# Windowed attention with sinks and a maxout FFN on one core: row-tiled scores, values by one head, transposes by DMA, and one ring of eight PSUM banks

## The chip, the cores and the metric

The kernel runs on one core of a Trainium2 chip. The metric is the device time of one execution in microseconds (us), as the median of a few runs. The engines are called TensorE (PE in the profile, its weight loads PEld), VectorE (DVE), ScalarE (ACT), GpSimd (POOL) and SyncE (SP, which only issues DMAs here).

## The reference

There are 4 batches, 8 heads, 768 positions and 64 numbers per head. Each query sees the 128 positions up to its own and the first four positions (the sinks). The attention's output goes through an FFN whose hidden layer is the largest of three products.

```python
scores = (1.0 / np.sqrt(D)) * np.matmul(q, k.transpose(0, 1, 3, 2))
pos = np.arange(S)
rel = pos[:, None] - pos[None, :]
keep = (pos[None, :] < 4) | ((rel >= 0) & (rel < 128))
scores = np.where(keep, scores, -1000000000.0)
a = np.exp(scores - np.max(scores, axis=-1, keepdims=True))
a = a / (np.sum(a, axis=-1, keepdims=True) + 1e-09)
x = np.matmul(a, v).transpose(0, 2, 1, 3).reshape(4 * 768, 512)
h = np.maximum(np.maximum(x @ w1, x @ w2), x @ w3)      # 512 -> 768
out = h @ w_out                                         # 768 -> 512
```

All inputs and the output are float32. The kernel computes in bfloat16 with sums in float32.

## The kernel before

The work is cut into 12 chunks of 256 positions, three in each batch, so chunks 0, 3, 6 and 9 begin a batch. A chunk's attention reads its own keys and values and the last 128 of the chunk before. Chunks that begin a batch need neither those nor the sinks. Four pairs of heads are handled in a chunk.

`load` (L59) fetches a chunk of Q, K and V in float32 on SP's queue: four DMAs of 256 KB for Q and K (L70) and four of 128 KB for V (L75). GpSimd casts them to bfloat16 (L167 for Q and K, L175 for V); the first two chunks of Q and K are cast by VectorE. `prep` transposes Q or K of two pairs of heads on TensorE (L192); ScalarE copies the transposed Q out of PSUM (L195) and VectorE the transposed K (L200), with small copies for the sinks' keys (L208).

K is kept padded. The 128 columns of a stationary tile are 64 keys of one head and 64 of the other, and each head's 64 rows are zero in the other's half. `zeros` (L94 to L99) clears these halves, and those of V, mostly on GpSimd. With it one matmul of 128 rows gives the scores of both heads of a pair for 64 keys each. `score` (L222 to L226) makes two such tiles for a pair, ScalarE takes the exponentials (L232), and VectorE multiplies by a mask of zeros and ones (L234). Scores of the sinks (L240, L244) of all heads are made in one tile with the keys padded in the same way.

`av` multiplies these by V with a column of ones, so that the last column is the sum of the weights (L253 for the sinks, L263 for the rest, 130 columns for two heads). VectorE divides (L268 the reciprocal, L271 the product). `xpose` transposes the result on TensorE (L282) and ScalarE copies it (L283). `ffn_h` makes a tile of 256 hidden numbers for one of the three weight matrices in eight matmuls (L294). The first matrix is copied by ScalarE (L298); VectorE takes the maximum with the other two (L300). `ffn_y` makes 128 rows of the output in six matmuls of 512 columns (L305), ScalarE copies (L308), and SP stores.

PSUM has eight banks in three pools: two for scores, two for transposes and values, and four for the FFN. The order of all work is written out by hand as a string of steps, where K, Q, S, Z, A, T, F and Y stand for the functions above and the letter after them for the chunk:

```python
for i in range(2, NCH):
    if i + 2 < NCH:
        cast(i + 2)
    if i + 3 < NCH:
        load(i + 3)
    run("Sb0 Fa0 Sb1 Kc0 Fa1 Sb2 Kc1 Fa2 Sb3 Fa3 Zb Sb4 Fa4 Ab00 Sb5 Fa5 Ab01 Sb6 Qc0 Fa6 "
        "Sb7 Qc1 Fa7 Fa8 Ab10 Ab11 Ya0 Tb0 Tb1 Ya1", a=i, b=i + 1, c=i + 2)
```

So an iteration holds the FFN of one chunk, the attention of the next and the transposes of Q and K of the one after. The attention of chunks 0 to 2 and the FFN of chunks 0 and 1 stand ahead of the loop, in the same manner. The weights are loaded with a cast by DMAs on GpSimd's queue (`load_w`, L129, and `load_wo`, L138), in program order with GpSimd's other work.

Of the kernel before, what the change touches and what calls it, by code (L numbers as in the profile page):

```python
# [16 lines left out]
def kernel(  # L17
# [31 lines left out]
    with tc.manual_schedule():  # L49
# [3 lines left out]
        ps_s = tc.alloc_tile_pool(name="ps_s", bufs=2, space=bass.MemoryType.PSUM)  # L53
        ps_o = tc.alloc_tile_pool(name="ps_o", bufs=2, space=bass.MemoryType.PSUM)
        ps_f = tc.alloc_tile_pool(name="ps_f", bufs=4, space=bass.MemoryType.PSUM)

        raws = {}

        def load(ci, gate=None):  # L59

            b, c = divmod(ci, CPB)
            t0 = c * 256
            eng = nc.sync
            qk = raw.tile([128, 2, H, 2, D], F32, tag="qk_raw", name="qk_raw")
            vr = raw.tile([128, 2, NP, 2, D], F32, tag="v_raw", name="v_raw")
            if gate is not None:
                gate.memset(qk[0:1, 0, 0, 0, 0:1], 0.0)
            for g in range(2):
                for j, src in ((0, k), (1, q)):
                    eng.dma_start(  # L70
                        out=qk[:, j, 4 * g:4 * g + 4],
                        in_=src[b, 4 * g:4 * g + 4, t0:t0 + 256].rearrange("h (p i) d -> p h (i d)", i=2))
            for h in range(2):
                for n in range(2):
                    eng.dma_start(  # L75
                        out=vr[64 * h:64 * h + 64, n],
                        in_=v[b, h::2, t0 + 128 * n:t0 + 128 * n + 128]
                            .rearrange("a (r i) d -> r a (i d)", i=2))
            raws[ci] = (qk, vr)

        load(0)
        vs_raw = const.tile([H * n_sink, B, D], F32, name="vs_raw")
        for h in range(H):
            nc.sync.dma_start(out=vs_raw[h * n_sink:(h + 1) * n_sink],
                              in_=v[:, h, 0:n_sink].rearrange("b s d -> s b d"))


        kb_sb = [const.tile([128, CPB, 2, NP, 2, 128], BF16, name=f"kb{i}") for i in range(2)]
        qT = [const.tile([128, NP, S], BF16, name=f"qT{i}") for i in range(2)]
        vb_sb = [const.tile([128, CPB, 2, NP, 2, 2, D + 1], BF16, name=f"vb{i}") for i in range(2)]  # L90
        ks = [const.tile([128, NP * 136], BF16, name=f"ks{i}") for i in range(2)]
        vs = const.tile([128, B, H, D + 1], BF16, name="vs")

        def zeros(i, c, eng):  # L94
            for h in range(2):
                hp = slice(64 * h, 64 * h + 64)
                eng.memset(kb_sb[i][hp, c, :, :, :, 64 - 64 * h:128 - 64 * h], 0.0)  # L97
                eng.memset(vb_sb[i][hp, c, :, :, :, 1 - h], 0.0)
                eng.memset(vb_sb[i][hp, c, :, :, :, h, D:D + 1], 1.0)  # L99

        zeros(0, 0, nc.vector)
        nc.vector.memset(ks[0], 0.0)
        nc.vector.memset(ks[1], 0.0)

        ident = const.tile([128, 128], BF16, name="ident")
        make_identity(nc, ident)

        msk = const.tile([128, 2, 4, 128], BF16, name="msk")
        nc.gpsimd.memset(msk[:, :, 0:2], 1.0)
        for h in range(2):  # L110
            hp = slice(64 * h, 64 * h + 64)
            nc.gpsimd.affine_select(
                out=msk[hp, :, 1], in_=msk[hp, :, 1], compare_op=ALU.is_ge, fill=0.0,
                base=0, pattern=[[-1, 2], [1, 128]], channel_multiplier=-2)
            nc.gpsimd.affine_select(
                out=msk[hp, :, 0], in_=msk[hp, :, 0], compare_op=ALU.is_gt, fill=0.0,
                base=0, pattern=[[1, 2], [-1, 128]], channel_multiplier=2)
        nc.gpsimd.tensor_copy(msk[:, :, 2:4], msk[:, :, 0:2])
        msk0 = const.tile([128, 2, 3, 128], BF16, name="msk0")
        nc.gpsimd.tensor_copy(msk0, msk[:, :, 1:4])  # L120
        for h in range(2):
            nc.gpsimd.memset(msk0[64 * h:64 * h + n_sink // 2, :, 0:2], 1.0)

        w_sb = {}

        def load_w(fo, fn):
            for wi, w in enumerate((moe_w1, moe_w2, moe_w3)):
                wt = const.tile([128, DS, fn], BF16, name=f"w{wi}_{fo}")
                nc.gpsimd.dma_start(  # L129
                    out=wt, in_=w[:, fo:fo + fn].rearrange("(a p) f -> p a f", p=128))  # L130
                for f in range(fn // 128):
                    w_sb[wi, fo // 128 + f] = wt[:, :, f * 128:(f + 1) * 128]
# [3 lines left out]
        def load_wo():  # L136
            for a in range(2):
                nc.gpsimd.dma_start(  # L138
                    out=wo[:, 3 * a:3 * a + 3],
                    in_=moe_w_out[384 * a:384 * a + 384].rearrange("(a p) f -> p a f", p=128))  # L140


        R = H * n_sink
        bm = const.tile([R, H], F32, name="bm")

        def sink_v_init():
            nc.gpsimd.memset(bm, 1.0)
            nc.gpsimd.affine_select(out=bm, in_=bm, compare_op=ALU.is_ge, fill=0.0, base=0,
                                    pattern=[[-n_sink, H]], channel_multiplier=1)
            nc.gpsimd.affine_select(out=bm, in_=bm, compare_op=ALU.is_ge, fill=0.0,  # L150
                                    base=n_sink - 1, pattern=[[n_sink, H]], channel_multiplier=-1)
            nc.gpsimd.memset(vs, 0.0)

        def sink_v(b):
            nc.gpsimd.tensor_tensor(
                out=vs[0:R, b, :, 0:D],
                in0=vs_raw[:, b].unsqueeze(1).to_broadcast([R, H, D]),
                in1=bm.unsqueeze(2).to_broadcast([R, H, D]), op=ALU.mult)
            nc.gpsimd.tensor_copy(vs[0:R, b, :, D:D + 1], bm.unsqueeze(2))

        bfs = {}

        def cast_qk(ci, j, g, eng):
            qk = raws[ci][0]
            if ci not in bfs:
                bfs[ci] = raw.tile([128, 2, 2, 2, 256], BF16, tag="qk_bf", name="qk_bf")
            eng.tensor_copy(  # L167
                bfs[ci][:, j, g].rearrange("p i (h d) -> p h i d", d=D),
                qk[:, j, 4 * g:4 * g + 4])

        def cast_v(ci, h):
            b, c = divmod(ci, CPB)
            vr = raws[ci][1]
            hp = slice(64 * h, 64 * h + 64)
            nc.gpsimd.tensor_copy(  # L175
                vb_sb[b % 2][hp, c, :, :, :, h, 0:D].rearrange("p n a i d -> p (n a i) d"),
                vr[hp].rearrange("p n a i d -> p (n a i) d"))

        def cast(ci):
            for j, g in ((0, 0), (1, 0), (0, 1), (1, 1)):  # L180
                cast_qk(ci, j, g, nc.gpsimd)
            for h in range(2):
                cast_v(ci, h)

        def prep(ci, j, g):

            b, c = divmod(ci, CPB)
            x = bfs[ci]
            pt = ps_o.tile([128, 2, 2, 128], BF16, tag="o", name="pt")
            for i in range(2):  # L190
                for p in range(2):
                    nc.tensor.transpose(pt[:, i, p], x[:, j, g, i, p * 128:(p + 1) * 128], ident)  # L192
            if j == 1:
                dst = qT[b % 2][:, 2 * g:2 * g + 2, c * 256:c * 256 + 256]
                nc.scalar.copy(dst.rearrange("p a (t i) -> p i a t", i=2), pt)  # L195
            else:
                kb = kb_sb[b % 2]
                for h in range(2):
                    hp = slice(64 * h, 64 * h + 64)
                    nc.vector.tensor_copy(  # L200
                        kb[hp, c, :, 2 * g:2 * g + 2, :, 64 * h:64 * h + 64]
                            .rearrange("p i a n r -> p i (a n) r"),
                        pt[hp].rearrange("p i a (n r) -> p i (a n) r", r=64))
                if c == 0:
                    kv = ks[b % 2].rearrange("p (a y) -> p a y", y=136)
                    for h in range(2):
                        for i in range(2):
                            nc.vector.tensor_copy(  # L208
                                kv[:, 2 * g:2 * g + 2, 4 * h + i:4 * h + 4:2],
                                kb[:, 0, i, 2 * g:2 * g + 2, 0, 64 * h:64 * h + 2])  # L210

        es = {}

        def score(ci, s):
            b, c = divmod(ci, CPB)
            p, i = divmod(s, 2)
            kb = kb_sb[b % 2]
# [161 lines left out]
        for i in range(2, NCH):  # L379
            if i + 2 < NCH:  # L380
                cast(i + 2)
# [42 lines left out]
```

## Time and profile before

| What | Value |
|---|---|
| median of 3 runs | 237.17 us (236.94 to 238.38) |
| profiled execution: span | 235.6 us |
| TensorE busy | 203.3 us, 86% |
| VectorE, ScalarE, GpSimd busy | 140.4, 115.1, 91.8 us |
| DMA | 28.66 MB, 122 GB/s over the span |

The span is the time from the first to the last instruction of the profiled execution, and the median holds what lies around it too, so the two differ by 1.6 us. Busy shares are means over stages that have different limits: the start, where weights and the first chunks arrive, the loop over chunks, and the last chunk. Matmuls are pipelined, so the mean length of one holds its latency, and the distance from one to the next is shorter.

### The profile page before, as it was taken

How to read it: one execution, taken by the hardware profiler on the slowest of the kernel's cores; microseconds unless marked ns; L12 is line 12 of the kernel's file. 1: busy time of each engine (PE TensorE's matmuls, PEld its weight loads, DVE VectorE, ACT ScalarE, POOL GpSimd, SP SyncE). 2: the span in 40 equal slices, each digit the busy share in tenths (PEclk: the TensorE clock that was granted, in tenths of full speed). 3: DMA queues.
4: the chain of work that ended last, by engine and by line, in shares of the span. 5: the costliest groups of instructions: out<-in, count | busy, mean ns of one | idle time of the engine just before them, and what ended most of it. 6: DMA issues, size and time to landing. Idle time of an engine off the chain costs nothing.

```text
span 235.6 us, 4953 instructions
## 1 busy us (share of the span) xinstructions
PE 203.3 (86%) x1956; PEld 163.9 (70%) x1968; DVE 140.4 (60%) x314; ACT 115.1 (49%) x213; POOL 91.8 (39%) x129
## 2 busy tenths in 40 slices
PE   0647876989944999999899999998999999999993
PEld 0434655877533868978778869877978689799781
DVE  7737674456342973855856739729629648547350
ACT  2622363257450457546446555464564466473411
POOL 8599961699468650621602502603404300000000
PEclk9999999999997999999999999999999999999998
DMA  6599199682699904907607519139039020010202
GB/s 171 101 134 239 32 161 259 118 120 58 182 278 233 232 18 142 218 3 234 122 22 236 105 63 266 30 101 251 10 107 248 4 89 4 25 66 0 92 0 89
DMA packets 46006, 28.66 MB, mean 122 GB/s; under 512 B 2208, under 2 KB 42912, under 8 KB 45984
## 3 DMA queue, kind: packets, MB, share of 16 engines
q1 hardware_dynamic: 42016, 25.21, 43.4%
q0 software_dynamic: 3968, 3.15, 9.0%
q8 instruction: 15, 0.25, 0.5%
q14 instruction: 7, 0.06, 0.1%
HBM read 25.20 MB, written 6.29 MB: 134 GB/s over the span
## 4 chain that ended last, share of the span: by engine, by line
PE 57%; DVE 13%; POOL 9%; DMA 7%; ACT 5%; issue 4%; SPq 3%; POOLq 0%; DVEq 0%; ACTq 0%
PE h_ps L294 29%; PE y_ps L305 10%; PE o_ps L263 6%; DMA v_raw<-in_v_dram 4%; DVE e_sb L234 4%; DVE h_sb L300 4%; DMA w<-in_moe_w_dram 3%; PE st L224 3%; ACT e_sb L232 3%; PE pt L192 2%; DVE kb L200 2%; PE xt_ps L282 2%; POOL vb L175 2%; SPq L70 2%; POOL kb L97 2%
## 5 line engine op out<-in xcount | busy, mean ns | idle before, releaser
L294 PE MATMUL h_ps<-xT,w 128*128 128x256 bf16 x864 | 111.0, 278 | 2.2 <-DMA w<-in_moe_w_dram 1.5
L294 PEld LDWEIGHTS <-w 128*128 128x128 bf16 x864 | 82.7, 100 | 13.1 <-DMA w<-in_moe_w_dram 2.0
L232 ACT ACTIVATE e_sb<-st 128x512 bf16<-128x512 f32 (+1 forms) x96 | 53.5, 564 | 44.2 <-PE st L226 44.2
L234 DVE TENSOR_TENSOR e_sb<-e_sb,msk 128x1024 bf16<-128x1024 bf16 (+1 forms) x48 | 36.6, 762 | 56.0 <-ACT e_sb L232 55.9
L300 DVE TENSOR_TENSOR h_sb<-h_sb,h_ps 128x512 bf16<-128x512 bf16 x72 | 49.3, 685 | 15.6 <-PE h_ps L294 13.3
L167 POOL CAST qk_bf<-qk_raw 128x512 bf16<-128x512 f32 x40 | 24.9, 627 | 82.0 <-DMA qk_raw<-in_k_dram 71.1
L263 PE MATMUL o_ps<-vb,e_sb 128*128 128x130 bf16 x352 | 30.8, 227 | 6.8 <-DVE e_sb L234 4.0
L305 PE MATMUL y_ps<-wo,h_sb 128*128 128x512 bf16 x132 | 32.7, 379 | 0.6
L263 PEld LDWEIGHTS <-e_sb 128*128 128x128 bf16 x352 | 24.8, 100 | 10.5 <-DVE e_sb L234 6.2
L308 ACT COPY y_sb<-y_ps 128x512 f32<-128x512 f32 x24 | 14.0, 585 | 35.6 <-PE y_ps L305 32.1
L175 POOL CAST vb<-v_raw 64x1024 bf16<-64x1024 f32 x24 | 26.5, 1104 | 9.5 <-DMA v_raw<-in_v_dram 6.1
L192 PE MATMUL pt<-ident,qk_bf 128*128 128x128 bf16 x192 | 19.4, 230 | 12.1 <-DVE qk_bf L167 5.5
L298 ACT CAST h_sb<-h_ps 128x512 bf16<-128x512 f32 x36 | 21.1, 585 | 15.8 <-PE h_ps L294 15.6
L224 PE MATMUL st<-qT,kb 128*128 128x256 bf16 x96 | 27.0, 285 | 1.6 <-ACT qT L195 0.8
L200 DVE COPY kb<-pt 64x512 bf16<-64x512 bf16 x48 | 20.1, 419 | 6.9 <-PE pt L192 6.3
L192 PEld LDWEIGHTS <-qk_bf 128*128 128x128 bf16 x192 | 13.6, 102 | 14.4 <-POOL qk_bf L167 7.1
L195 ACT COPY qT<-pt 128x512 bf16<-128x512 bf16 x24 | 17.7, 737 | 11.5 <-PE pt L192 11.5
L226 PE MATMUL st<-qT,kb 128*128 128x128 bf16 x96 | 21.9, 228 | 0.0
L271 DVE TENSOR_TENSOR x_sb<-o_ps,rc 128x256 bf16<-128x256 f32 x48 | 20.4, 425 | 1.7
L305 PEld LDWEIGHTS <-h_sb 128*128 128x128 bf16 x144 | 13.0, 98 | 11.9 <-DVE h_sb L300 1.2
L283 ACT COPY xT<-xt_ps 128x512 bf16<-128x512 bf16 x24 | 13.2, 595 | 9.0 <-PE xt_ps L282 9.0
L222 PE MATMUL st<-qT,kb 128*128 128x128 bf16 x64 | 14.0, 218 | 0.9 <-ACT qT L195 0.8
(43 smaller groups left out, 130.7 us busy)
## 6 DMA issues: line engine op xcount, KB each, us to landing
qk_raw<-in_k_dram SPq DMA_DIRECT2D x24, 256.0 KB
qk_raw<-in_q_dram SPq DMA_DIRECT2D x24, 256.0 KB
v_raw<-in_v_dram SPq DMA_DIRECT2D x48, 128.0 KB
out_dram<-y_sb SPq DMA_DIRECT2D x24, 256.0 KB
w<-in_moe_w_dram POOLq DMA_DIRECT2D x3, 512.0 KB, 7.4
w<-in_moe_w_dram POOLq DMA_DIRECT2D x3, 256.0 KB, 4.9
wo<-in_moe_w_out_dram POOLq DMA_DIRECT2D x2, 384.0 KB, 5.6
vs_raw<-in_v_dram SPq DMA_DIRECT2D x8, 4.0 KB
```

Of the source, the lines that this page charges most:

```text
L167: eng.tensor_copy(bfs[ci][:, j, g].rearrange("p i (h d) -> p h i d", d=D), qk[:, j, 4 * g:4 * g + 4])
L175: nc.gpsimd.tensor_copy(vb_sb[b % 2][hp, c, :, :, :, h, 0:D].rearrange("p n a i d -> p (n a i) d"), vr[hp].rearrange("p n a i d -> p (n a ...
L192: nc.tensor.transpose(pt[:, i, p], x[:, j, g, i, p * 128:(p + 1) * 128], ident)
L200: nc.vector.tensor_copy(kb[hp, c, :, 2 * g:2 * g + 2, :, 64 * h:64 * h + 64] .rearrange("p i a n r -> p i (a n) r"), pt[hp].rearrange("p i ...
L224: nc.tensor.matmul(st[:, 1:3], lhsT=kb[:, c, i, p, 0], rhs=qh[:, q0:q0 + 256], start=True, stop=True)
L226: nc.tensor.matmul(st[:, 3], lhsT=kb[:, c, i, p, 1], rhs=qh[:, q0 + 128:q0 + 256], start=True, stop=True)
L232: nc.scalar.activation(e[:, i, lo:], st[:, lo:], AF.Exp, scale=scale)
L234: nc.vector.tensor_mul(e[:, :, lo:], e[:, :, lo:], msk if c > 0 else msk0)
L263: nc.tensor.matmul(o[:, 2 * a:2 * a + 2], lhsT=es[ci, p][:, i, sl], rhs=vb_sb[b % 2][:, n // 2, n % 2, p, i], start=(c == 0 and x == 0), s ...
L294: nc.tensor.matmul(hp[:, f], lhsT=w_sb[wi, 2 * fp + f][:, ds], rhs=xTs[ci][:, ds, :], start=(ds == 0), stop=(ds == DS - 1))
L300: nc.vector.tensor_max(dst, dst, hp)
L305: nc.tensor.matmul(yp, lhsT=hs[ci][:, fb, t * 128:(t + 1) * 128], rhs=wo[:, fb], start=(fb == 0), stop=(fb == FB - 1))
```

## The change

The kernel is written anew on the same chunks. Its parts:

- **Layout.** Each DMA of Q, K or V takes a whole chunk (512 KB). A partition holds two neighbouring positions. K and Q are kept without padding, transposed, in rings of four chunks (`kT`, `qT`), V in a ring of four (`vb`).
- **Scores.** For each head of a pair a matmul uses 64 rows of TensorE (rows 0 to 63 or 64 to 127) and gives 128 keys of one head. The two heads' matmuls alternate and write to two banks.
- **Values.** A matmul covers 128 keys of one head and has 65 columns. Four tiles of PSUM (one for each pair) are held open through a chunk's values, both halves of 128 queries in one tile.
- **Sinks.** Their scores are four matmuls on 32 columns of TensorE each, their values matmuls on 32 rows each. The sinks' V is gathered by a matmul with a selection matrix (`sink_v`), no longer by DMAs.
- **Transposes.** Q and K of chunks 0 to 2 and x of chunks 0 to 2 go through TensorE. From chunk 3 on, Q and K are transposed by four DMAs a chunk (`turn_dma`) and x by one (`xpose_dma`), all on SP's queue.
- **PSUM.** One pool of eight banks serves every tile in turn.
- **Start.** Loads of chunks 0 and 1 are issued at once (Q of chunk 0 on ScalarE's queue), each weight matrix is one DMA, and the masks are built in half the size first.
- **Stores.** A chunk is stored by two DMAs.

```diff
-        ps_s = tc.alloc_tile_pool(name="ps_s", bufs=2, space=bass.MemoryType.PSUM)
-        ps_o = tc.alloc_tile_pool(name="ps_o", bufs=2, space=bass.MemoryType.PSUM)
-        ps_f = tc.alloc_tile_pool(name="ps_f", bufs=4, space=bass.MemoryType.PSUM)
+        psum = tc.alloc_tile_pool(name="psum", bufs=8, space=bass.MemoryType.PSUM)
+        def bank(shape, dtype, name):
+            return psum.tile(shape, dtype, tag="b", name=name)
+        RING = 4
+        kT = [const.tile([128, 2, NP, 2, 64], BF16, name=f"kT{i}") for i in range(RING)]
+        qT = [const.tile([128, 2, NP, 2, 64], BF16, name=f"qT{i}") for i in range(RING)]
+        vb = [const.tile([128, 2, H, D + 1], BF16, name=f"vb{i}") for i in range(RING)]
...
+        def turn_dma(ci, w):
+            dst = (kT if w == "k" else qT)[ci % RING]
+            x = bfs[ci, w].rearrange("q p i a d -> q (p i a d)")
+            for n in range(2):
+                nc.sync.dma_start_transpose(
+                    out=dst[:, n].rearrange("q p i r -> q (p i) r"), in_=x[64 * n:64 * n + 64])
...
+        def score(ci, pairs):
+            b, c = divmod(ci, CPB)
+            kc, qc = kT[ci % RING], qT[ci % RING]
+            for p in pairs:
+                st = [bank([128, 4, 128], F32, "st") for a in range(2)]
+                for s, x, n, q0, q1 in ((0, kT[(ci - 1) % RING], 1, 0, 1), (1, kc, 0, 0, 2),
+                                        (3, kc, 1, 1, 2)):
+                    if s == 0 and c == 0:
+                        continue
+                    for a in range(2):
+                        hp = slice(64 * a, 64 * a + 64)
+                        nc.tensor.matmul(
+                            st[a][:, s:s + q1 - q0],
+                            lhsT=x[hp, n, p].rearrange("q i r -> q (i r)"),
+                            rhs=qc[hp, q0:q1, p].rearrange("q n i r -> q n (i r)"),
+                            start=True, stop=True)
...
+        def expo(ci, p):
+            lo = 0 if ci % CPB else 1
+            e, st = es[ci, p]
+            for a in range(2):
+                nc.scalar.activation(e[:, a, lo:], st[a][:, lo:], AF.Exp, scale=scale)
+            nc.vector.tensor_mul(e[:, :, lo:], e[:, :, lo:], msk0 if lo else msk)
...
+        def av_open(ci):
+            b, c = divmod(ci, CPB)
+            for p in range(NP):
+                os_[ci, p] = bank([128, 2, 2, D + 1], F32, "o")
+            if c:
+                for t in range(2):
+                    for p in range(NP):
+                        hp = slice(32 * p, 32 * p + 32)
+                        nc.tensor.matmul(
+                            os_[ci, p][:, t], lhsT=es[ci, "sink"][hp, t], rhs=vs[b % 2][hp],
+                            start=(t == 0), stop=False, skip_group_check=True,
+                            tile_position=(32 * p, 0))
...
+                    for s, cv, n in blocks:
+                        nc.tensor.matmul(
+                            o[:, t, a], lhsT=e[:, a, s], rhs=vb[cv % RING][:, n, 2 * p + a],
+                            start=first, stop=True, skip_group_check=True)
+                        first = False
...
+        def xpose_dma(ci):
+            xTs[ci] = work.tile([128, 2, DS, 128], BF16, tag="xT", bufs=3, name="xT")
+            nc.sync.dma_start_transpose(
+                out=xTs[ci].rearrange("q t s r -> q (t s) r"),
+                in_=xs[ci].rearrange("q t p a d -> q (t p a d)"))
...
+        masks()
+        for g in range(2):
+            for w in "kq":
+                cast_qk(0, w, g, nc.vector)
+                turn(0, w, g)
+            score(0, range(2 * g, 2 * g + 2))
+            for p in range(2 * g, 2 * g + 2):
+                expo(0, p)
...
+        load_w(0)
+        load_w(1)
+        sink_init()
+        sink_k(0)
+        masks_late()
+        for g in range(2):
+            cast_qk(1, "k", g, nc.vector)
+            cast_qk(1, "q", g, nc.gpsimd)
+        load_w(2)
...
+        load_wo()
+        av_open(0)
...
+        cast(3)
+        load(4)
+        for p in range(NP):
+            expo(2, p)
+            if p < 2:
+                ffn_y(0, p)
+        store(0)
+        turn_dma(3, "k")
+        turn_dma(3, "q")
...
         for i in range(2, NCH):
+            n = i + 1
+            last = n >= NCH
+            cast(i + 2)
+            load(i + 3)
+            if i + 2 < NCH:
+                turn_dma(i + 2, "k")
+                turn_dma(i + 2, "q")
+            if not last:
+                if n % CPB == 1:
+                    sink_k(n // CPB)
+                    sink_v(n // CPB)
+                sink_score(n)
+                score(n, range(NP))
+                expo(n, 0)
+            ffn_y(i - 1, 0)
+            if not last:
+                expo(n, 1)
+            ffn_y(i - 1, 1)
+            store(i - 1)
+            if not last:
+                expo(n, 2)
+            ffn_h(i, 0, 0)
+            if not last:
+                expo(n, 3)
+            ffn_h(i, 0, 1)
+            ffn_h(i, 0, 2)
+            if not last:
+                av_open(n)
+                av(n, 0)
+            ffn_h(i, 1, 0)
...
+            if not last:
+                av(n, 3)
+                xpose_dma(n)
+            for wi in range(3):
+                ffn_h(i, 2, wi)
+        for t in range(2):
+            ffn_y(NCH - 1, t)
+            store(NCH - 1, t, t + 1)
```

## The prediction

> **What bounds the kernel now.** I read the page's busy shares first, then the 40 slices.
>
> ```profile
> PE 203.3 (86%) x1956; PEld 163.9 (70%) x1968; DVE 140.4 (60%) x314; ACT 115.1 (49%) x213; POOL 91.8 (39%) x129
> ...
> PE   0647876989944999999899999998999999999993
> ...
> DMA  6599199682699904907607519139039020010202
> ```
>
> There are two stages. From about the thirteenth slice (74 us) TensorE is full; before that it has holes. The stretches of the loop (columns: TensorE, weight loads, VectorE, ScalarE, GpSimd busy; clock; DMA share; GB/s) show the full part; the first is a chunk whose next attention chunk has sinks, the second one without (chunk 6):
>
> ```profile
> 106.30:123.70 17.40, 16.60 (x175) 14.04 (x175) 10.88 (x30) 9.70 (x19) 4.95 (x6) 1.00 0.49 123
> 123.70:139.70 16.00, 15.23 (x151) 12.19 (x151) 10.37 (x22) 8.78 (x18) 4.56 (x6) 1.00 0.54 142
> ```
>
> No engine but TensorE is near full there, and its clock is whole. The loop starts at 73.8 us and its last iteration at 221.4, so nine iterations take 147.6 us, 16.4 each. The last iteration and the tail take 14.2. The chain of waits explains the first 74 us and gives the pace of matmuls (start, length, what):
>
> ```profile
> 28.36 0.75 POOL w L129
> 29.11 7.38 DMA w<-in_moe_w_dram
> 36.54 1.06 PE h_ps L294 x8
> ...
> 98.10 0.46 PE o_ps L263 x8
> 99.00 0.87 PE h_ps L294 x8
> ```
>
> The second part of the weights is issued at 28.4 us because GpSimd clears padding and prepares sinks first; a second hole (69 to 74 us) is a late load. For the pace: eight 256-column matmuls take 0.87 us, 0.109 each, and eight of 130 columns 0.46, 0.057 each. The means in the groups hold the latency too and must not be multiplied by the count. The other rows I use are these (busy, mean ns of one):
>
> ```profile
> L232 ACT ACTIVATE e_sb<-st 128x512 bf16<-128x512 f32 (+1 forms) x96 | 53.5, 564 | 44.2 <-PE st L226 44.2
> L300 DVE TENSOR_TENSOR h_sb<-h_sb,h_ps 128x512 bf16<-128x512 bf16 x72 | 49.3, 685 | 15.6 <-PE h_ps L294 13.3
> L308 ACT COPY y_sb<-y_ps 128x512 f32<-128x512 f32 x24 | 14.0, 585 | 35.6 <-PE y_ps L305 32.1
> L271 DVE TENSOR_TENSOR x_sb<-o_ps,rc 128x256 bf16<-128x256 f32 x48 | 20.4, 425 | 1.7
> ...
> q1 hardware_dynamic: 42016, 25.21, 43.4%
> q0 software_dynamic: 3968, 3.15, 9.0%
> ```
>
> The queue line gives a rate: 25.21 MB in 43.4% of 235.6 us is 247 GB/s, and 39 ns for a packet on one of 16 engines. All weights cost 9.0%, 21.2 us.
>
> **TensorE's work for one chunk, before and after.** Before, at the paces above (128 columns 0.057): FFN 72 x 0.109 = 7.85; y 12 x 0.215 = 2.6; scores 8 x (0.057 + 0.109 + 0.057) = 1.8; values 32 x 0.057 = 1.8; sinks 8 x 0.11 = 0.9; transposes of Q and K 16 x 0.057 = 0.9; of x 8 x 0.057 = 0.45. The sum is 16.3, which is the 16.4 measured, so a chunk was matmul columns and nothing else. After: FFN and y stay. The 24 transposes go (-1.35). The scores keep their 32 matmuls, now on 64 rows, two beside each other in two banks; no row shows that pairing, so they cost between 0.9 (paired) and 1.8 (one after the other). The value matmuls keep their number with 65 columns; between 0.028 (columns halve) and 0.057 (the weight load sets the pace): I take 0.044, 1.4 us. Sinks, in four tiles: 0.2 to 0.9, I take 0.6. The work is then about 13.6 (12.4 to 15.5). Off other engines go the copies of K (two of 0.42, and ks copies, per half), Q (0.74) and x (0.6), and GpSimd's clearing of padding.
>
> The Trainium skill ("TensorEngine Tiling (Array Packing)", section "Key Properties") says that a change of tiling mode drains TensorE. Scores, sinks and sink values have three modes, so four changes a chunk; at the 0.23 us that a 128-column matmul takes alone in the groups that would be an estimated 0.9 us a chunk or 8 us in all if none lay in a wait.
>
> **But the new order does not let TensorE run dense.** I walk one iteration of the loop, from its first score at 0, with ScalarE's exponentials of 512 columns following each other every 0.5 us (a pair in 1.09), VectorE's masks 0.75, maxima 0.69, a reciprocal with its product 0.60, and 0.17 us of matmul latency. All tiles come in turn from eight banks, so a tile waits for the reader of the tile eight before it. Scores fill eight banks, 0 to 1.2. ScalarE does the first pair by 1.6; y's first half takes the bank freed first, 1.2 to 2.5, and its copy 2.7 to 3.3 stands ahead of the second pair in ScalarE's queue (4.3). y's second half ends on TensorE at 3.8, its copy at 4.8, the third pair at 5.85, the first h copy at 6.35, the fourth pair at 7.4. TensorE has done three h tiles by 6.5 and then waits until 7.45, since the output banks of the values are those of the third and fourth pair. Then sinks 0.4, four value groups of 0.35 and six h tiles of 0.87 bring it to 14.5, with the next sink scores 14.65. VectorE has masked the fourth pair at 8.2 and works without a pause to 15.3; x is complete at 13.4. The next scores start at 14.65, their last pair when the last maximum frees a bank (15.35), which no one waits for. The period is 14.65. Without sinks the exponentials are 384 columns (0.4 apart): 13.1. Six of the first and three of the second: 127.2 us for the nine iterations, against 147.6. Pairing of the scores matters little here, since TensorE waits for ScalarE in that half anyway.
>
> **Moved to DMA.** SP's queue in an iteration holds three loads, four transposes of K and Q for two chunks on, two stores, and the transpose of x; each waits for those ahead of it. Copies: 1.57 MB of loads and 0.52 of stores are 8.5 us at 247 GB/s. Transposes move 0.79 MB more, and no row shows one. Lower bound: the bytes at the copy rate, 3.2 us. Upper: a packet for every run of 64 (K, Q) or 128 elements (x) of a destination row, 4096 + 1024 packets x 39 ns / 16 = 12.5 us. Further off, a packet for each element would be 960 us a chunk. I take the lower: the rows read and the rows written are whole lines of 1 to 2 KB, as in the store rows. Then 11.7 of 14.1 us are DMA and hidden. If that cover is gone, the iteration is as long as its DMA. K and Q have a whole iteration to land. x has less: its transpose is issued at 13.4 and the next iteration's first h tile wants it at 14.65 + 3.9, so 5.1 us. A 256 KB load was issued at 107.57 and its reader started at 110.76: 3.2 us. It fits by 2 us. Each us beyond 5.1 delays the h tile, its copy, and the fourth pair behind it on ScalarE: 9 us in all.
>
> The Trainium skill speaks against this step: "VectorE: DVE Perf Modes", section "The three transpose paths", has 1309 ns for a 128x128 block by DMA and 390 ns on TensorE, and advises TensorE. If 24 blocks a chunk went one after another at that, an estimate of 31 us a chunk, the time would be some 355 us. "DMA: Bandwidth & Descriptors", section "Latency and other measured facts", has 261 GB/s for the transpose instead, by which the sum stays. No run here shows either.
>
> **The start.** GpSimd no longer clears padding; it casts v, then issues whole weight matrices, the first at about 11.5 us (10.5 before) and the third at about 19 (28.4 to 29.8 for the second parts before). Its queue still holds the sinks' set-up and the masks, and q's cast, ahead of the third; VectorE and TensorE wait for q's cast, not for long. So DMA is never empty, and the loop's first score waits for the transposed K and Q of chunk 3, which stand on SP behind the load of chunk 4 and one store. Sum: five loads of 1.57 MB at 247 GB/s 31.9, weights 21.2, a store 2.1, K and Q 2.1, first issue 0.8: 58 us. TensorE's own work until there is about 35 us. Ends: 50 if load 4 comes behind them, 73.8 as before.
>
> **Sum.** 58 + 127.2 + the last iteration (y 2.6, h 7.85, y 2.6, copy and store 3.5 as between 232.1 and 235.6) 16.6 = 202 us of span. The profiled span is 235.6 and the median of the runs 237.17, 1.6 more: 203.4.
>
> **Rivals.** Slower: the transposes are bound by their packets. Price 12.5 us a chunk, 21 with the copies: 58 + 189 + 16.6 + 1.6 = 265. It decides from 18 us of DMA an iteration, that is 9.5 us for the transposes of a chunk (83 GB/s), or from 9 us between x's issue and its landing. For it: nothing in this trace transposes by DMA, and blocks of 64 rows are small. Against it: whole lines on both sides. Chance 0.28.
>
> The ring of banks takes back what TensorE gains: each bank hand-over costs some 0.2 us more than walked, and the iteration is 16.4 again: 58 + 147.6 + 16.6 + 1.6 = 224. For it: values and scores hold twelve banks an iteration of a ring of eight. Against it: ScalarE has 8.1 us and VectorE 9.5 of work in 14.65. Chance 0.10.
>
> It doesn't do what it says: 64-row matmuls don't pair and 65 columns take as long as 130. TensorE then has 15 us a chunk, but 0.9 of it lies in the wait; second half +0.4 to 0.9: 208 to 211, a case inside the forecast.
>
> The start stays as it was (73.8) with a better loop: 219. Chance 0.05.
>
> **How the numbers follow.** The forecast has 0.57: 203 us, its own range 190 (start 50, iterations 13.4) to 213. To it come 219, 224 and a part of the slow transposes; up to 256 about 0.15 is left out above, 0.05 below 190. About 1% can be told from no change here. Faster by more than that: 0.57 + 0.10 + 0.05, less a little for mixtures, 0.70; slower 0.28; the same 0.02.
>
> **What would show it.** Right: loop iterations of 14 to 15 us with 13 where no sinks follow; ScalarE back to back while TensorE waits some 1 us ahead of the values; transposes of x landing in 3 to 5 us; loop start at 55 to 62 us; DMA share near 0.8. Wrong: the first h tile of an iteration waiting for xT, scores waiting for qT or kT from DMA, DMA full through the loop, or transposes of K and Q landing an iteration late.

## The result and the profile after

The changed kernel takes 204.6 us in the median of four runs (202.84 to 206.73), against 237.06 for the kernel before beside it: a ratio of 0.861, interval 0.853 to 0.868. The prediction was 203. Run again on another chip it took 203.7 (0.860, 0.855 to 0.864). The profiled execution is the longest of the four, with a span of 205.0 us, a time of 206.73 and a granted clock of 0.958, and the ratios here and below are taken without such slow runs.

The page of the changed kernel, busy shares, slices and queues:

```profile
PE 174.1 (85%) x1788; PEld 129.8 (63%) x1800; DVE 111.5 (54%) x239; ACT 88.9 (43%) x177; POOL 71.9 (35%) x139
...
PE   0345978999739999999967999999999899999990
...
PEclk9999995799976999999997999999999999999999
DMA  5999999993569829979999989789899963142404
...
q1 hardware_dynamic: 68992, 31.73, 74.1%
q0 software_dynamic: 2368, 3.15, 9.9%
```

TensorE has 29 us less work, and the loop starts earlier. The line of DMA is the new thing: before, it had holes all along the loop; now it is near full through the 32nd slice (164 us), but for a pause at 46 to 61 us and one short one at 74. The stretches of the loop (columns as in the prediction: span, five engines, clock, DMA share, GB/s):

```profile
75.20:89.00 13.80, 13.73 (x162) 10.40 (x160) 9.52 (x20) 7.20 (x15) 5.26 (x8) 1.00 1.03 192
89.00:102.80 13.80, 12.84 (x145) 9.77 (x143) 8.97 (x20) 6.97 (x14) 5.22 (x8) 1.00 1.01 194
102.80:119.40 16.60, 14.16 (x131) 10.49 (x132) 8.60 (x19) 6.03 (x13) 5.20 (x10) 0.90 1.05 206
119.40:133.90 14.50, 14.05 (x176) 10.84 (x175) 9.80 (x20) 8.29 (x17) 5.72 (x8) 1.00 0.98 200
133.90:146.10 12.20, 12.15 (x130) 9.32 (x132) 7.91 (x17) 5.87 (x12) 5.75 (x8) 1.00 1.03 206
```

The second and third of these hold the same chunks as the two of before: 17.4 us became 13.8, but 16.0 became 16.6. The cuts are rough. The one at 133.9 lies inside a chunk's scores, as TensorE's timeline shows (sk are the sinks' scores, o the values; the line of ACT is the fourth pair's exponentials):

```profile
119.19 0.28 PE L231 MATMUL sk<-qT,ks 128*32 128x256 bf16 x4
...
125.39 1.17 ACT L222 ACTIVATE e_sb<-st 128x512 bf16<-128x512 f32 x2
126.03 0.42 PE L277 MATMUL o<-vb,e_sb 128*128 128x65 bf16 x8
...
132.34 0.29 PE L231 MATMUL sk<-qT,ks 128*32 128x256 bf16 x4
...
146.03 0.78 PE L210 MATMUL st<-qT,kT 64*128 64x256 bf16 x13
```

From first score to first score, and to the last chunk's y at 186.6, the nine iterations take 14.4, 13.5, 14.3, 16.4, 13.2, 13.7, 13.3, 14.2 and 13.1 us. The first began at a low clock (0.83 from 60.5 to 75.2). The longest has no sinks, which should have made it short. The chain of waits says why (start, length, what):

```profile
99.86 2.82 DMA qT<-q_bf
103.06 5.67 DMA xT<-x_sb
108.77 4.40 PE h_ps L314 x24
...
155.70 3.47 DMA qT<-q_bf
159.17 5.08 DMA xT<-x_sb
164.30 2.79 PE h_ps L314 x24
...
173.85 0.99 PE st L210 x24
```

Scores wait for qT; right behind them the FFN waits for x's transpose. The second costs twice: after the wait that ends at 108.8 us, 24 matmuls take 4.40 us where they take 2.79 behind the one that ends at 164.3, and the granted clock of that stretch is 0.90. The waits are no matter of this one execution: with another order on ScalarE (below), at a clock of 0.983, the FFN waits 5.4 us in four places for x's transpose. The timeline of SP's queue (start, length of issue) in the iteration ahead shows where the transposes stood:

```profile
88.49 1.33 SPq L301 DMA_TRANSPOSE xT<-x_sb  x1
89.88 0.60 SPq L81 DMA_DIRECT2D k_raw<-in_k_dram  x1
90.53 0.60 SPq L81 DMA_DIRECT2D q_raw<-in_q_dram  x1
91.23 1.39 SPq L81 DMA_DIRECT2D v_raw<-in_v_dram  x1
92.72 5.77 SPq L117 DMA_TRANSPOSE kT<-k_bf  x2
98.58 2.54 SPq L117 DMA_TRANSPOSE qT<-q_bf  x2
101.22 1.28 SPq L338 DMA_DIRECT2D out_dram<-y_sb  x2
103.06 1.61 SPq L301 DMA_TRANSPOSE xT<-x_sb  x1
```

SP issues without a pause from 88.5 to 102.5 us. The two transposes of K take 5.8 us to issue, behind a load of 1.57 MB; Q's follow, then two stores, and only then x's next transpose. So SP comes round once in 14.6 us, while TensorE has 12.9 us of work (summed below). The median landing times of the three transposes are these (columns: issues, us from issue to landing):

```profile
kT<-k_bf SPq DMA_TRANSPOSE x18, 4.4
qT<-q_bf SPq DMA_TRANSPOSE x18, 3.0
xT<-x_sb SPq DMA_TRANSPOSE x9, 3.3
```

### The profile page after: what moved, and what is told of

Read it like the earlier page. It is cut to its first block, busy times and chain, and to the rows that moved or that the text cites. A ratio compares the mean times of both kernels' runs of the same rounds, so it can differ in the third digit from the quotient of the medians.

```text
span 205.0 us, 4504 instructions
## 1 busy us (share of the span) xinstructions
PE 174.1 (85%) x1788; PEld 129.8 (63%) x1800; DVE 111.5 (54%) x239; ACT 88.9 (43%) x177; POOL 71.9 (35%) x139
## 3 DMA queue, kind: packets, MB, share of 16 engines
q1 hardware_dynamic: 68992, 31.73, 74.1%
## 4 chain that ended last, share of the span: by engine, by line
PE 48%; DMA 14%; ACT 11%; DVE 10%; issue 8%; SPq 4%; POOL 2%; DVEq 0%
PE h_ps L314 30%; PE y_ps L331 8%; ACT e_sb L222 7%; DMA xT<-x_sb 5%; DMA qT<-q_bf 4%; PE st L210 4%; DVE h_sb L322 3%; DMA q_raw<-in_q_dram 3%; DVE x_sb L285 3%; SPq L117 3%; PE pt L106 2%; PE o L277 2%; DMA k_raw<-in_k_dram 2%; ACT y_sb L333 2%; DVE e_sb L223 2%
## 5 line engine op out<-in xcount | busy, mean ns | idle before, releaser
L314 PEld LDWEIGHTS <-w 128*128 128x128 bf16 x864 | 83.6, 100 | 17.4 <-DMA xT<-x_sb 5.0
L322 DVE TENSOR_TENSOR h_sb<-h_sb,h_ps 128x512 bf16<-128x512 bf16 x72 | 49.2, 683 | 18.6 <-PE h_ps L314 16.4
L91 POOL CAST k_bf<-k_raw 128x512 bf16<-128x512 f32 x20 | 13.4, 694 | 70.6 <-issue 42.0
L96 POOL CAST vb<-v_raw 64x512 bf16<-64x512 f32 x48 | 31.2, 650 | 10.6 <-DMA v_raw<-in_v_dram 8.6
L331 PEld LDWEIGHTS <-h_sb 128*128 128x128 bf16 x144 | 13.7, 100 | 17.9 <-issue 3.9
L333 ACT COPY y_sb<-y_ps 128x512 f32<-128x512 f32 x24 | 14.2, 592 | 21.8 <-PE y_ps L331 11.0
L285 DVE TENSOR_TENSOR x_sb<-o,rc 128x256 bf16<-128x256 f32 x48 | 20.4, 425 | 1.7
L277 PE MATMUL o<-vb,e_sb 128*128 128x65 bf16 x352 | 18.7, 197 | 1.7 <-DVE e_sb L223 1.7
L210 PE MATMUL st<-qT,kT 64*128 64x128 bf16 (+1 forms) x256 | 15.0, 256 | 4.7 <-DMA qT<-q_bf 2.3
L277 PEld LDWEIGHTS <-e_sb 128*128 128x128 bf16 x352 | 16.3, 100 | 4.1 <-DVE e_sb L223 2.2
L91 POOL CAST q_bf<-q_raw 128x512 bf16<-128x512 f32 x22 | 14.8, 699 | 3.6 <-DMA q_raw<-in_q_dram 3.4
L210 PEld LDWEIGHTS <-kT 64*128 64x128 bf16 x256 | 10.3, 101 | 8.4 <-issue 7.0
L296 PE MATMUL xt<-ident,x_sb 128*128 128x128 bf16 x24 | 4.3, 280 | 4.9 <-DVE x_sb L285 4.8
L282 DVE RECIPROCAL rc<-o 128x4 f32<-128x4 f32 x48 | 8.4, 175 | 0.1
L297 ACT COPY xT<-xt 128x512 bf16<-128x512 bf16 x6 | 3.2, 588 | 11.7 <-PE xt L296 11.7
```

The costliest lines, as they stand in the source:

```text
L91: eng.tensor_copy(x[:, 2 * g:2 * g + 2].rearrange("q p i a d -> q p a i d"), y[:, 4 * g:4 * g + 4].rearrange("q (p a) i d -> q p a i d", a=2))
L96: eng.tensor_copy(vb[ci % RING][64 * i:64 * i + 64, n, :, 0:D], raws[ci, "v"][64 * n:64 * n + 64, :, i])
L210: nc.tensor.matmul(st[a][:, s:s + q1 - q0], lhsT=x[hp, n, p].rearrange("q i r -> q (i r)"), rhs=qc[hp, q0:q1, p].rearrange("q n i r -> q n ...
L277: nc.tensor.matmul(o[:, t, a], lhsT=e[:, a, s], rhs=vb[cv % RING][:, n, 2 * p + a], start=first, stop=True, skip_group_check=True)
L285: nc.vector.tensor_mul(xs[ci][:, :, p], o[:, :, :, 0:D], rc.unsqueeze(3).to_broadcast([128, 2, 2, D]))
L314: nc.tensor.matmul(hp[:, f].rearrange("q (t r) -> q t r", t=2), lhsT=w_sb[wi][:, ds, c0:c0 + 128], rhs=xTs[ci][:, :, ds], start=(ds == 0), ...
```

## The experiments

The theory after this reading was that the transposes cost DMA more than forecast and that DMA, with SP's queue, sets the pace of the seven iterations that load. The rival was the prediction's own walk: ScalarE's order sets it.

**K and Q transposed twice.** A second copy goes to a scratch tile.

```diff
+            for n in range(2):
+                nc.sync.dma_start_transpose(
+                    out=scr[ci % 2][:, n].rearrange("q p i r -> q (p i) r"), in_=x[64 * n:64 * n + 64])
```

> Each transpose of K and Q by DMA is issued a second time, into a scratch tile that nobody reads; nothing else changes. Theory 1 (the loop's full iterations are as long as their DMA): the after trace has 9 to 10 tenths of DMA from 60 to 160 us; the transposes cost about 5.8 us of the 16 engines a chunk, two thirds of it K and Q, so 3.9 us more for each of nine chunks: some 35 us, 235 to 245 us. Theory 2 (as predicted: ScalarE's order sets the period and the transposes are hidden): the doubled ones still fit at 3.2 us a chunk, and the time grows by 0 to 3 us.

Measured: 250.14 us (ratio 1.061, 1.054 to 1.067), 45.5 us more, or 5.05 for each of nine chunks: above what the first theory gave, far above the second. The costliest group, with the idle time before it and what ended it, names x's transpose:

```profile
L319 PE MATMUL h_ps<-xT,w 128*128 128x256 bf16 x864 | 105.6, 277 | 22.9 <-DMA xT<-x_sb 22.9
```

Scores wait another 21.8 us for qT. So there is no room for more transposes in the loop. Four more issues are also 5.0 us of SP, so this run alone does not tell DMA from SP.

**All transposes on TensorE.** `turn` and `xpose` serve all chunks, and no DMA transposes anything.

```diff
-                turn_dma(i + 2, "k")
-                turn_dma(i + 2, "q")
...
+                turn(i + 2, "k", 0)
+                turn(i + 2, "q", 0)
...
-                xpose_dma(n)
...
+                xpose(n, 0)
+                xpose(n, 1)
```

> The DMA transposes are undone: Q, K and x of every chunk go through TensorE, with their copies by VectorE and ScalarE, as chunks 0 to 2 do. Theory 1: DMA falls to 8.5 us an iteration and binds nowhere; TensorE's 12.8 us a chunk become 14.2, so the loop is about as long as before the undoing, 200 to 208 us, and TensorE is dense. Theory 2: transposes by DMA cost nothing, so undoing them costs at least the 1.35 us of TensorE and part of the copies for each of nine chunks: 215 to 220 us.

Measured: 209.9 us (0.891, 0.886 to 0.896), between the theories. Its iterations but the last are 14.4 to 15.0 us and dense:

```profile
L314 PE MATMUL h_ps<-xT,w 128*128 128x256 bf16 x864 | 105.3, 275 | 0.0
...
q1 hardware_dynamic: 39904, 24.65, 46.4%
```

The FFN's matmuls, which waited 3.2 us in the changed kernel, wait for nothing here. The DMA transposes are thus worth some 5 to 7 us net of their stalls. The queue line is what prices them below: 46.4% of a span of 207.7 is 96.4 us without transposes.

**x alone on TensorE.**

```diff
-                xpose_dma(n)
...
+                xpose(n, 0)
+                xpose(n, 1)
```

> Only x goes back to TensorE; K and Q stay on DMA. Theory 1: a third of the transposes leaves the DMA queues (14.3 us an iteration become 12.4), and nobody waits behind SP's queue for xT; TensorE gains 0.45 us a chunk. The iterations become as long as the ScalarE walk, 13 to 14 us: 196 to 203 us. Theory 2: 0.45 us of TensorE more in nine chunks and nothing saved: 206 to 209 us.

Measured: 205.3 us (202.6 to 206.0; 0.863, 0.856 to 0.871), no difference from the changed kernel that can be measured. Waits for xT are gone and the mean iteration is 13.8 us, but 0.45 us of transposes a chunk are back on TensorE. In time it decides nothing; its queue line serves below.

**Exponentials ahead of y's copies.** All four pairs follow each other on ScalarE.

```diff
-                expo(n, 0)
+                for p in range(NP):
+                    expo(n, p)
```

> In the loop all four exponentials of a chunk stand ahead of the copies of y on ScalarE (TensorE's order is the same). Theory 1: while DMA is full nothing is won; only the two iterations after the last load get shorter by 1 us: 200 to 204 us. Theory 2: TensorE's wait ahead of the values goes, 1 us in each of the six iterations with sinks: 196 to 199 us.

Measured: 204.0 us (0.865, 0.860 to 0.871). No gain that can be measured, so ScalarE's order isn't what bounds the changed kernel. The last interval between two chunks' y, where no loads disturb, is 11.75 us here and 11.74 with the old order (in the second run of the changed kernel): the wait that the prediction had walked to isn't seen there.

**Chunk 3's K and Q transposed ahead of the store and a load.**

```diff
+        turn_dma(3, "k")
+        turn_dma(3, "q")
         load(4)
...
         store(0)
-        turn_dma(3, "k")
-        turn_dma(3, "q")
```

> The four transposes of Q and K of chunk 3 stand on SP ahead of the load of chunk 4 and of the store of chunk 0 (before, behind both). Theory A (the prediction's sum of bytes: the DMA engines set the start): the bytes ahead of them fall by 1.57 and 0.52 MB, and the loop's first score comes at about 50 us instead of 60.5: 195 to 198 us. Theory B (from the after trace: DMA is half empty from 46 to 56 us, and SP waits for ScalarE's copies of y ahead of the store): the transposes go out at about 50 us, when the casts of chunk 3 are done, the first score comes when TensorE has done its own work, at 57.5 to 58.5, and 2 to 3 us are won: 201 to 203 us.

Measured: 204.2 us (199.7 to 206.4). The loop's first score comes at 58.5 us instead of 60.5 and no longer waits for qT; a gain in the total isn't told from the spread of the runs. The 50 us of the first theory is refuted; some 2 us of the start is all that this order held back.

**Scores of one head, then the other.** The two loops are swapped, so that a head's three matmuls follow each other.

```diff
-                for s, x, n, q0, q1 in (...):
-                    for a in range(2):
+                for a in range(2):
+                    for s, x, n, q0, q1 in (...):
```

> The scores of a pair are issued first for one head and then for the other, so that neighbours on TensorE use the same 64 rows. If the alternation is what lets two run beside each other, the 24 matmuls of a chunk take 1.7 us or more instead of 1.0 to 1.1. As the prediction has it (that half of the iteration waits for ScalarE) the time stays: 203 to 206 us. If TensorE's columns bind (rival), it grows by 0.8 us in each of twelve chunks: 212 to 214 us.

Measured: 203.5 us (0.864, 0.860 to 0.868). From this kernel's chain of waits:

```profile
171.27 1.00 PE st L210 x24
```

The changed kernel had 0.99 for the same 24 matmuls. They hold 4096 columns, 1.75 us one after the other at the pace of the FFN's (24 matmuls of 256 columns in 2.62 us). The likely reading is that two heads run beside each other in either order. That a matmul of 64 rows takes half the time by itself isn't excluded. The experiment didn't undo the pairing, and what pairing is worth stays open.

**Q by one transpose of 128 rows.** The tile's order becomes pair, half, block, row, so that one DMA does what two of 64 rows did.

```diff
-        qT = [const.tile([128, 2, NP, 2, 64], BF16, name=f"qT{i}") for i in range(RING)]
+        qT = [const.tile([128, NP, 2, 2, 64], BF16, name=f"qT{i}") for i in range(RING)]
...
+            if w == "q":
+                nc.sync.dma_start_transpose(
+                    out=qT[ci % RING].rearrange("q p i n r -> q (p i) (n r)"), in_=x)
+                return
```

> Q is laid out so that one DMA of 128 rows transposes it, as x is, instead of two of 64 rows; the bytes are the same, K is unchanged. In the runs so far K and Q cost 4.6 to 4.9 us of the 16 engines a chunk for 0.52 MB, and x 1.3 us for 0.26 MB. Theory A (a transpose costs by its blocks of rows: 64 rows cost nearly as much as 128): Q falls from 2.4 to 1.3 us a chunk, the DMA queue's share of time falls by about 10 us in all, and the time by 4 to 8 us as far as TensorE lets it: 197 to 201 us. Theory B (a transpose costs by its bytes, and K and Q only look dear because loads run beside them): nothing changes, 203 to 206 us.

Measured: 200.4 us (0.844, 0.838 to 0.849), 3 to 4 us less than the changed kernel. The blocks of 64 rows are a part of the price. This takes off both DMA time and one SP issue of 1.25 us, and doesn't part the two.

**Two versions that put these together.** The first has Q wide, K on TensorE, exponentials first and chunk 3 early. The second keeps K's two transposes by DMA (K's stationary tile needs its 128 keys side by side, so it stays in blocks of 64) and is otherwise the same.

```diff
-                turn_dma(i + 2, "k")
...
+                turn(i + 2, "k", 0)
...
+                    turn(i + 2, "k", 1)
```

> All of it together: Q by one DMA of 128 rows, K back on TensorE, x by DMA, the exponentials ahead of y's copies, and the transposes of chunk 3 early. DMA needs 8.5 + 2.6 us an iteration and TensorE 12.8 to 13.2. If DMA was what bound the loop and TensorE's columns come next, nine iterations take 115 to 120 us instead of 127, and the time is 192 to 197 us. If ScalarE's or VectorE's order binds, or the transposes by DMA come late for another reason than their amount, it stays above 200.

> As the combined kernel, but K stays on DMA (two transposes of 64 rows a chunk). Two limits are set against each other: DMA 8.5 + 1.3 + 1.3 + 2.4 = 13.5 us in the seven iterations that have loads, TensorE 12.3 to 12.6. If DMA binds there, these iterations take 13.5 and the last two 11.8 to 12.5, and nine take 119 us, the same as in the combined kernel (118.6 to 119.6): 198 to 200 us. If TensorE binds, they take 112 us: 191 to 193 us.

Measured: 198.7 us (0.844, 0.841 to 0.848) with K on TensorE, and **196.35 us (193.9 to 197.8; 0.828, 0.823 to 0.833) with K by DMA**, the fastest kernel of this study and 7.3 us below the changed kernel on the same chip. Its first iteration and three later ones, here cut at y's first matmul:

```profile
59.38:73.71 14.33, 14.10 (x140) 10.21 (x140) 9.73 (x19) 6.51 (x15) 5.44 (x10) 0.88 0.66 116
...
86.86:99.81 12.95, 12.82 (x140) 9.75 (x141) 9.23 (x18) 6.74 (x14) 5.24 (x8) 1.00 1.15 222
99.81:112.46 12.65, 12.60 (x142) 9.83 (x141) 8.64 (x19) 6.13 (x15) 5.17 (x10) 1.00 1.07 219
112.46:125.61 13.15, 13.08 (x154) 10.10 (x153) 8.96 (x18) 6.95 (x15) 4.78 (x8) 1.00 1.20 221
```

TensorE is idle for at most 0.13 us in each of the later ones, and 12.65 to 13.15 us is the bare work of a chunk. So TensorE binds there, as the second limit of the expectation has it; the total is 3 us above the 191 to 193 that went with it, and the first iteration, at a clock of 0.88, is 14.33. DMA's share is above 1 here, though TensorE waits for no DMA: the times of packets overlap, so a share of 1 isn't a hard limit. The changed kernel carried the same bytes at 192 to 206 GB/s and this one at 219 to 222.

**The first weight matrix ahead of V's casts**, on the version with K on TensorE.

```diff
+        load_w(0)
...
-        load_w(0)
```

> The combined kernel with the first weight matrix issued ahead of the casts of V on GpSimd's queue, at 5 us instead of 11.5. Theory A (the bytes set the start, whatever their order): the weights come earlier and chunk 1 later, and the loop's first score stays at 58 to 60 us: 198 to 200 us. Theory B (the first hidden tiles, which wait for these weights at 25.5 us, set the start): they move up by as much as 5 us and the loop's start by 2 to 5: 193 to 197 us.

Measured: 200.2 us (0.848, 0.844 to 0.853), with the loop's first score at 60.5 us instead of 58.8. This order of the bytes at the start doesn't help.

**The changed kernel again**, beside the last two.

> The changed kernel once more, unaltered, on the chip of the two above, so that their differences can be read against it: 203 to 206 us, with nine iterations of the loop in 126 to 128 us.

Measured: 203.7 us, as told above.

**Transposes of K and Q ahead of the load** in each iteration.

```diff
-            load(i + 3)
             if i + 2 < NCH:
                 turn_dma(i + 2, "k")
                 turn_dma(i + 2, "q")
+            load(i + 3)
```

> In each iteration the four transposes of K and Q stand ahead of the load on SP's queue instead of behind it; nothing else differs from the changed kernel. Theory A (order): the late qT comes from the 1.5 MB load that is issued ahead of its transpose, so that scores and then x wait at 103 and 159 us though DMA has capacity left. Then no scores wait for qT in the loop, the issue of K's two transposes falls from 3.7 to 5.8 us to about 2.5, the two long iterations (16.6 and 13.9 us) come down to some 13.3, and the time is 198 to 201 us. Theory B (capacity): an iteration holds 14.7 us of DMA whatever its order, the wait goes to the last transfer in the new order (x's transpose, behind the load and the stores, landing in 5 us or more), iterations with loads stay at 14.2 on average, and the time is 202 to 206 us.

Measured: 215.2 us (0.910, 0.907 to 0.914), which neither theory gave. Two steps of the first came true. K's issue falls to 2.6 us, as SP's timeline shows, and qT makes no scores wait inside the loop:

```profile
86.81 2.59 SPq L117 DMA_TRANSPOSE kT<-k_bf  x2
89.50 3.11 SPq L117 DMA_TRANSPOSE qT<-q_bf  x2
92.66 0.58 SPq L81 DMA_DIRECT2D k_raw<-in_k_dram  x1
```

Then something that neither had named is late. TensorE's timeline (the bracket holds the idle time ahead and its releaser):

```profile
72.50 0.29 PE L231 MATMUL sk<-qT,ks 128*32 128x256 bf16 x4 [0.95 <-POOL ks L180]
...
117.56 0.40 PE L231 MATMUL sk<-qT,ks 128*32 128x256 bf16 x4 [4.09 <-POOL ks L180]
...
119.72 4.05 PE L331 MATMUL y_ps<-wo,h_sb 128*128 128x512 bf16 x12
...
134.41 2.76 PE L331 MATMUL y_ps<-wo,h_sb 128*128 128x512 bf16 x12
...
165.42 0.41 PE L231 MATMUL sk<-qT,ks 128*32 128x256 bf16 x4 [5.63 <-POOL ks L180]
```

GpSimd copies a batch's sink keys (L180) behind the casts of a chunk, in program order, and the casts wait for the load. With the load later, the copy is later, and the first sink scores of each batch wait 0.95, 4.09 and 5.63 us, 10.7 in all; in the changed kernel the second of these copies was done 1.9 us ahead of its reader. Behind the wait of 4.09 us twelve y matmuls take 4.05 us where they otherwise take 2.76. The three iterations free of such a wait and of the slow stretch behind it are 13.2 to 13.4 us long, with their load. So the load ahead of the transposes did hold them up, and its place in front was what kept GpSimd's work in time. A version with the copy ahead of the casts wasn't tried.

**The price of the transposes** comes out of the queue lines: q1's share times the span, on kernels that differ in what DMA transposes.

| Transposed by DMA | q1's share x span | us |
|---|---|---|
| nothing | 46.4% x 207.7 | 96.4 |
| K and Q in blocks of 64 rows | 69.9% x 200.9 | 140.4 |
| K, Q and x (mean of five executions, 151.9 to 157.9) | e.g. 74.1% x 205.0 | 154.6 |
| K in blocks, Q wide, x (two kernels) | 73.7% x 199.2, 76.3% x 194.3 | 146.8, 148.2 |
| Q wide, x | 64.9% x 196.6 | 127.6 |
| K, Q and x, K and Q ahead of the load (the last run) | 67.1% x 212.3 | 142.5 |

By ninths (nine chunks): K and Q 44.0/9 = 4.9 us, x 14.2/9 = 1.6, together 6.5; Q wide saves 0.8. But the same transfers come to 46.1/9 = 5.1 us together in the order of the last run. So these are the times of packets that share the engines with others, not fixed prices.

## Why the prediction was right, and where it wasn't

The time was right, and so were its three stages. The reasons for the middle one were only half right.

**The sum.** Start 60.6 us (58 forecast), nine iterations 126.0 (127.2), the rest 18.4 (16.6): 205.0 of span against 201.8, in the longest of four executions.

**The nine iterations hold by cancelling.** Forecast were three of 13.1 without sinks and six of 14.65 with them. Measured are 14.4, 16.4 and 13.3 for the three, 4.8 us more, and 13.1 to 14.3 for the six, 6.0 less in all. The excess is the low clock of the first and the late transposes of the second; the gain is TensorE's cheaper work and a wait that didn't come. That the two nearly cancel is luck.

**TensorE's work** was taken as 13.6 us a chunk. At the chain's paces it is 72 FFN matmuls 7.85, y 2.6, scores 1.07, values 32 x 0.030 = 0.96, sink scores 0.22 and sink values 0.22: 12.9. The term that was most too dear is the values: 65 columns take 0.030 us, the lower end of what was given, not 0.044. Scores came out at the paired end. (The prediction counts 32 score matmuls a chunk; with sinks there are 24 in either kernel, as its own sum for before has it. Its upper end of 15.5 doesn't follow from its terms, which add up to 14.95.) The fastest kernel's iterations of 12.65 to 13.15 agree with the sum. The drain at a change of tiling mode, of which "TensorEngine Tiling (Array Packing)", "Key Properties", in the Trainium skill tells, was put at an estimated 0.9 us a chunk. That is too much: ahead of the sinks' tiles 24 FFN matmuls take 2.71 us to the next start instead of 2.62, some 0.1 for a change into them.

**The walk along ScalarE** failed as the cause, though its times were good. In the iteration from 119.2 us ScalarE ends the fourth pair 7.4 us in, as walked. But the values begin 6.8 us in, and in the loop they never wait for exponentials. The step that failed is that the values' output banks would be those of the third and fourth pair and hold TensorE until 7.45. Which banks they had, no run shows. Reordering ScalarE gained nothing, and the iterations with neither a late transpose nor a low clock were 13.1 to 13.7 us.

**The transposes by DMA** are the mis-sized term: 3.2 us a chunk taken, 6.5 measured in the changed kernel's order and 5.1 in the last run's, between the bounds of 3.2 and 12.5. The step that failed was the argument that whole lines on both sides move at the copy rate. With the copies' 8.5 an iteration holds 15 us of packet time and not 11.7, against 12.9 of TensorE's work. The prediction had priced a lost cover ("the iteration is as long as its DMA"), and 14.1 us is the mean of the seven iterations that load. But that price isn't shown: by the same count the fastest kernel has 14.2 us of DMA (8.5 + 6.5 - 0.8) in iterations of 12.65 to 13.15, and the last run's three free iterations took 13.2 to 13.4. What lengthened the changed kernel's is what stood late in SP's order. The rival of packet-bound transposes began at 9.5 us a chunk, so the truth fell short of it by 3.

Of the pages of the Trainium skill that the prediction weighed, neither fits. The 1309 ns for a 128x128 block in "VectorE: DVE Perf Modes", "The three transpose paths", stand against 6.5/24 = 0.27 us of packet time for one of a chunk's 24 blocks. The 261 GB/s in "DMA: Bandwidth & Descriptors", "Latency and other measured facts", stand against 0.79 MB in 6.5 us of packet time, 121 GB/s, or in 5.1 us, 154 GB/s.

**"K and Q have a whole iteration to land"** was true of the order and false of the time: that iteration of SP's queue is itself 14 us long, and in two of nine iterations qT came after the scores wanted it. With the load behind them, in the last run, scores waited for qT nowhere in the loop, so the load in front was the cause.

**x's transpose** lands in 3.3 us in the median, as forecast. But its issue was walked from the moment x is complete, and SP was still issuing the stores behind Q's transposes then. In the long iteration x was complete at 101.7 us, its transpose was issued at 103.1 and landed 5.7 later, and the FFN had wanted it at 106.5. The one issued at 159.2 took 5.1.

So three of the marks that were named as wrong did appear: FFN tiles waiting for xT, scores waiting for qT, and DMA full through the loop. They cost 3.2 us of waits for xT and 0.9 for qT inside the loop (another 1.6 for qT stand ahead of it), plus a lower clock in one stretch, and what TensorE's cheaper work saved paid for them.

**The start.** "DMA is never empty" held until 46 us only. From 46 to 60.5 it moved 114 GB/s: SP held chunk 3's transposes behind a store, which waited for ScalarE's copies of y. Moving them ahead brought the loop's first score 2.0 us forward, moving the weights put it 1.8 us back. What sets the rest of the start between 46 and 58 us wasn't tested.

**Still open:** whether DMA's throughput or SP's time to issue was the tighter in the changed kernel. Doubling, widening and the fastest kernel changed both together. The last run changed only the order, but its free iterations stand among ones that waits had lengthened, in which both could catch up.

## What to carry to other kernels

When work moves from a full engine to DMA, price it as a queue as well as bytes: here a transfer was issued only after all that stood before it on SP, and the transfer that someone waits for should not stand behind the big load that no one needs yet. Before moving that load, follow everything on the other engines that stands behind its readers, since a small copy in such a queue (here 0.2 us of sink keys) can cost more than the move saves. A total that agrees with the forecast is no proof of its terms; the iterations one by one showed the errors that cancelled.

## What the runs showed of the hardware

A transpose by DMA of 256 KB took some 2.4 us of q1's time in blocks of 64 rows (K and Q, 4.9/2), 1.6 for x in one of 128 rows, beside the loads and stores of this loop. In another order of the queue all five of a chunk took 5.1 us instead of 6.5. SP needed 1.25 us to issue one against 0.6 for most loads, and up to 2.9 on average for K's two behind a full queue.

The 24 score matmuls of the two row halves took 0.99 us issued alternately and 1.00 three and three, where 4096 columns one after the other would be 1.75.

The granted clock is not only a matter of the start. After a wait of 4 us in the loop, y's twelve matmuls took 4.05 us against 2.76, at a clock of 0.63 from 117.5 to 124 us. In the start, the 72 FFN matmuls at 33 us took 10.44 against 7.86, at 0.75. But the length of the wait alone didn't decide it: with K and Q transposed twice, the FFN waited 3.4 us for xT at 84.8 us, and its 24 matmuls took 2.79 us behind it, as they do elsewhere.
